# A causal convolution of five taps: diagonal matmuls in split precision, or matmuls by quarters of 32 channels over a copy folded through DRAM

## The chip, the cores and the metric

The kernel runs on one core of a Trainium2 chip. Its engines are TensorE (PE; the loads of its weights are shown apart as PEld), VectorE (DVE), ScalarE (ACT), GpSimd (POOL), and SyncE (SP), which here only issues DMA transfers. The metric is the time of one execution in microseconds, as the median of several runs. Lower is better.

## The reference

Three layers over 4 sequences of 576 positions and 512 channels, all in fp32:

```
attention   8 heads of 64; scores q k^T / 8; only the 32 highest scores of a row are kept; softmax; times v
first MLP   h = relu(x w_in); u, v = halves of h; v normalized over its channels
            v = w_spatial v + b_spatial (over the positions);  x = (u * v) w_out
second MLP  g[s,c] = sum over k<5 of conv_w[k,c] * x[s-4+k,c]      (zeros before the start)
            out = (sigmoid(g) * (x w_val)) w_out2
```

The change is in the line for g: 5 taps along the positions, each channel by itself.

## The kernel before

Attention goes in 72 units of two tiles of 128 rows, 18 units for each sequence. A unit computes its scores on PE in two halves (L475), ACT copies each half out of PSUM (L478), DVE searches for the 32nd highest score of each row (L494 to L529, the longest part of a unit) and masks and sums (L546), ACT scales (L521, L554), PE transposes (L563, L568), ACT copies (L565, L570), and PE multiplies by v (L584). Up to three units of scores are buffered (`sb`).

The two MLPs of sequence b, called MoE b below, are listed with the attention of sequence b+1, so that PE works on them while DVE works on attention. MoE 3 has no attention beside it: it is the tail. Weights come as 64-bit floats, which are decoded at the start on ACT, DVE and POOL and put as two fp32r parts (a high and a low part) into DRAM (`w_...`); they are loaded by POOL into `wblk` when they are needed, 2 MB at a time. A product is three matmuls in fp32r: high by high, high by low, low by high (L625). Activations are split likewise: the high part on ACT (L609), the low part on POOL (L611).

Order on each engine: everything is put into a list with its dependencies, an engine and an estimated duration (`od.add`). `Order.play` plays this list by a priority, `Order.plan` plays it first with hand-set lead times (`AHEAD`), and then `ROUNDS` times from the end and from the start, and takes the play that it believes the shortest. Each engine then runs its instructions in that fixed order. So a change of an estimate or a dependency anywhere moves instructions everywhere.

The convolution, for MoE 0 to 2: `x2` (the input, `piece_x2`) is in `UX` as [128 channels, 4 blocks d, 4 + 576 positions] and split into `yh` and `yl`. For each half c of the positions and each block d, PE multiplies 15 times (L777): the high part of a diagonal matrix of tap k by `yh` and `yl`, its low part by `yh`, for 5 taps. The 40 diagonals are made once on ACT (L291, `diagonals`), and take the buffer `diag`, which the last sequence uses for a weight (`w_load_late`). ACT takes tanh(g/2) from PSUM into `gate` (L780). MoE 3, in the tail, does the convolution on DVE instead (L788); that part does not change.

Of the kernel before, what the change touches and what calls it, by code (L numbers as in the profile page):

```python
# [39 lines left out]
class Order:  # L40
# [7 lines left out]
    ROUNDS = 4  # L48
# [159 lines left out]
def attention_moe_pass(tc, sh, fast, qT, kT, v, w_in, w_spT, b_sp, w_out, w_val, conv_w, w_out2, out):  # L208
# [17 lines left out]
    with ExitStack() as ctx:  # L226
# [50 lines left out]
        cwp = [buf(f"cwp{z}", [128, KK * TAPS], dt) for z, dt in enumerate((F32R, F32))]  # L277
        DIAG = buf("diag", [128, 2, KK * TAPS, 128], F32R)

        def diagonals(od, at):  # L280

            flat = cw.rearrange("p k t -> p (k t)")
            od.add("ACT", 0.2, lambda: nc.scalar.activation(cwp[0], flat, AF.Copy), [("cw",)], [("cwp", 0)], at)
            od.add("POOL", 0.3, lambda: nc.gpsimd.tensor_tensor(cwp[1], flat, cwp[0].bitcast(F32), op=ALU.subtract),
                   [("cw",), ("cwp", 0)], [("cwp", 1)], at)
# [19 lines left out]
        def decode(od, st, src, n, at, w=None, name=None, kk=0, c=0):  # L305
# [8 lines left out]
            od.add("SP", fn=lambda: nc.sync.dma_start(raw, src), w=[(k, 0)], at=at, **dma(1, 1024 * n))  # L314
# [62 lines left out]
        def decode_all(od, jobs, stages, t0, t1):  # L377
            m = 0
            for z, (name, src, c, n, kk) in enumerate(jobs):
# [9 lines left out]
                else:  # L389
                    words = src.bitcast(I32)[kk * 128:(kk + 1) * 128, 2 * c:2 * (c + n)].rearrange("p (n t) -> p n t", t=2)  # L390
                    to = dict(name=name, c=c % DM) if name else dict(w=cw[:, kk, :])
# [14 lines left out]
        def w_load_late(od, name, at):  # L406

            t = DIAG.rearrange("p z j c -> p (z j c)")
            WT[name] = (t, ("wlate",))
            od.add("POOL", 1.05, lambda: nc.gpsimd.dma_start(t[:, 0:WN[name]], sh.scratch[name]), [("scr", name)],  # L410
                   [("wlate",)] + [("diag", z, d) for z in range(2) for d in range(KK)], at, 9.0)

        def wpart(t, lo):
            n = KK * FF
            return t[:, lo * n:lo * n + n].rearrange("p (k f) -> p k f", k=KK)
# [178 lines left out]
        mp_n, vr_n, ga_n, os_n = [0], [0], [0], [0]  # L594
# [32 lines left out]
        def moe(od, b, t0, t1):  # L627
# [131 lines left out]
            GJ = {}  # L759

            def conv(c, d, at):
# [6 lines left out]
                if b < B - 1:  # L768
                    j = nxt(mp_n, banks)
                    ps = MP[j]  # L770
                    ky = [k for r in region("y", d * YW + c0, d * YW + c1 + PADC) for k in r]

                    def go():
                        ops = [(z, y, k) for k in range(TAPS) for z, y in ((0, "yh"), (0, "yl"), (1, "yh"))]
                        ops.sort(key=lambda o: o[0])
# [64 lines left out]
            if b == B - 1:  # L840
                w_load_late(od, "out", ("L", PER * B))
                od.add("-", 0.0, lambda: None, [], [("sps",), ("ptp", 0), ("ptp", 1), ("xr",)] + [("mp", j) for j in range(NMP, banks)])
# [158 lines left out]
```

## Time and profile before

| | before |
|---|---|
| median of 3 runs | 843.98 us (842.83 to 844.89) |
| the profiled execution | 839.99 us, of which the span is 838.1 us |
| DVE busy in the span | 754.7 us (90%) |
| PE busy | 708.3 us (85%) |
| ACT busy | 602.8 us (72%) |
| POOL busy | 290.6 us (35%) |

The profiled execution is 3.99 us below the median of the runs shown. The stages by the trace: decoding and attention of sequence 0 until about 225 us, MoE 0 to 2 each beside the attention of the next sequence until about 742 us, and the tail (MoE 3) until 838 us.

### The profile page before, as it was taken

The page shows a single profiled execution, that of the slowest core. Times are in us where ns is not written, and L with a number is a line of the kernel's source. Part 1 is how long each engine was busy: PE and PEld are TensorE (multiplying, and loading weights), DVE is VectorE, ACT ScalarE, POOL GpSimd, SP SyncE. Part 2 cuts the span into 40 slices and gives each one's busy share as a digit, 9 for nine tenths or more (in the row PEclk, how much of TensorE's full clock was granted, in tenths as well). Part 3 has the DMA queues.
Part 4 walks back from the last instruction along what each step waited for, and adds up shares of the span by engine and source line. Part 5 has one row for each costly group of instructions (what it writes and reads, how often), then busy time and mean ns, then how long its engine had stood idle before and what let it go on. Part 6 is the DMA issues. An engine that isn't in the chain of part 4 may idle for free.

```text
span 838.1 us, 17270 instructions
## 1 busy us (share of the span) xinstructions
PE 708.3 (85%) x5969; PEld 605.2 (72%) x5969; DVE 754.7 (90%) x2749; ACT 602.8 (72%) x1390; POOL 290.6 (35%) x353
## 2 busy tenths in 40 slices
PE   3245545755899999998999999997999999999986
PEld 2234433544789899876888899875888999778985
DVE  6999999999999999999999999998989999951580
ACT  5668866777887777768977777786886777774341
POOL 4767255564523311132442322232333112322120
PEclk9955666777999999999999999998999999999999
DMA  7888332323134502153133412234035003533601
GB/s 248 245 261 304 101 121 91 115 86 109 39 100 146 184 2 76 55 196 120 29 134 113 156 30 102 100 101 143 2 142 194 23 2 131 210 120 123 221 2 61
DMA packets 46954, 99.25 MB, mean 118 GB/s; under 512 B 22532, under 2 KB 29960, under 8 KB 43272
## 3 DMA queue, kind: packets, MB, share of 16 engines
q0 software_dynamic: 4032, 53.74, 18.1%
q1 hardware_dynamic: 42824, 44.31, 16.8%
q8 instruction: 49, 0.80, 0.4%
q14 instruction: 49, 0.40, 0.2%
HBM read 79.88 MB, written 18.15 MB: 117 GB/s over the span
## 4 chain that ended last, share of the span: by engine, by line
DVE 51%; PE 23%; ACT 6%; issue 2%; POOL 1%; DMA 0%; POOLq 0%; DVEq 0%; ACTq 0%
DVE tw L527 10%; DVE e L546 10%; PE mp L625 8%; DVE t8b L529 7%; PE mp L728 4%; DVE tm L494 4%; DVE cand L503 4%; DVE tm L495 3%; DVE cand L506 3%; PE xr L584 3%; DVE t8a L516 2%; DVE cand L498 2%; PE sps L475 2%; DVE tn L499 2%; DVE gate L788 2%
## 5 line engine op out<-in xcount | busy, mean ns | idle before, releaser
L475 PE MATMUL sps<-k,q 64*128 64x144 f32 (+1 forms) x1280 | 126.4, 341 | 85.2 <-ACT sb L478 77.9
L475 PEld LDWEIGHTS sps<-k,q 64*128 64x128 f32 (+1 forms) x1280 | 90.4, 201 | 116.0 <-ACT sb L478 88.6
L546 DVE SCALAR_TENSOR_TENSOR e<-sb,t8b,e 128x576 f32<-128x576 f32 x144 | 132.5, 945 | 0.1
L529 DVE MAX8 t8b<-tw 128x8 f32<-128x168 f32 x432 | 120.3, 318 | 0.0
L554 ACT ACTIVATE e<-e,sums 128x576 f32<-128x576 f32 x144 | 106.6, 770 | 9.5 <-DVE sums L551 9.3
L521 ACT ACTIVATE e<-sb,neg 128x576 f32<-128x576 f32 x144 | 106.5, 770 | 2.2 <-PE ptp L563 1.0
L478 ACT ACTIVATE sb<-sps 128x576 f32<-128x576 f32 x144 | 93.0, 646 | 19.6 <-PE sps L475 17.2
L563 PE MATMUL ptp<-ident,e 128*128 128x128 f32 x576 | 94.5, 301 | 11.1 <-ACT e L554 8.5
L584 PE MATMUL xr<-pt,vt 128*64 128x128 f32 (+1 forms) x1280 | 87.8, 281 | 18.0 <-ACT pr L570 17.7
L625 PE MATMUL mp<-xh,wblk 128*128 128x288 f32 x448 | 102.2, 306 | 0.0
L584 PEld LDWEIGHTS xr<-pt,vt 128*64 128x64 f32 x1280 | 68.3, 144 | 36.4 <-ACT pr L570 23.6
L563 PEld LDWEIGHTS ptp<-ident,e 128*128 128x128 f32 x576 | 72.0, 153 | 25.0 <-ACT e L554 13.1
L527 DVE MATCH_REPLACE8 tw<-t8b,tw 128x168 f32<-128x168 f32 x288 | 88.8, 314 | 0.0
L565 ACT ACTIVATE pt<-ptp 128x512 f32<-128x512 f32 x144 | 81.7, 596 | 8.4 <-PE ptp L563 8.1
L625 PEld LDWEIGHTS mp<-xh,wblk 128*128 128x128 f32 x448 | 74.6, 188 | 5.5 <-issue 1.2
L625 PE MATMUL mp<-wblk,xh 128*128 128x512 f32 (+1 forms) x280 | 73.9, 406 | 1.1 <-POOL stage L327 1.1
L494 DVE TENSOR_TENSOR tm<-sb 128x576 f32<-128x576 f32 x72 | 58.8, 817 | 5.6 <-ACT sb L478 5.4
L611 POOL TENSOR_TENSOR yl<-ux,yh 128x288 fp32r<-128x288 f32 x31 | 29.5, 953 | 94.9 <-ACT yh L609 92.5
L625 PE MATMUL mp<-xl,wblk 128*128 128x288 f32 x224 | 60.9, 294 | 0.0
L625 PEld LDWEIGHTS mp<-wblk,xh 128*128 128x128 f32 (+1 forms) x280 | 49.8, 186 | 14.9 <-POOL stage L327 1.3
L495 DVE TENSOR_TENSOR tm<-sb 128x576 f32<-128x576 f32 x72 | 60.4, 838 | 0.0
L503 DVE MAX8 cand<-tm 128x8 f32<-128x288 f32 x144 | 57.8, 441 | 0.0
(180 smaller groups left out, 1687.9 us busy)
## 6 DMA issues: line engine op xcount, KB each, us to landing
wblk<-w_out POOLq DMA_DIRECT2D x7, 2048.0 KB, 8.4
wblk<-w_sp POOLq DMA_DIRECT2D x8, 1440.0 KB, 6.5
wblk<-w_inv POOLq DMA_DIRECT2D x4, 2048.0 KB, 8.3
wblk<-w_inu POOLq DMA_DIRECT2D x4, 2048.0 KB, 9.1
wblk<-w_val POOLq DMA_DIRECT2D x4, 2048.0 KB, 9.0
q<-in_qT SPq DMA_DIRECT2D x16, 288.0 KB, 3.9
k<-in_kT SPq DMA_DIRECT2D x16, 288.0 KB, 4.4
stage<-in_w_in SPq DMA_DIRECT2D x8, 512.0 KB, 4.5
```

The lines of the kernel that those rows point to most:

```text
L475: nc.tensor.matmul(dst[:, f:f + QUART], lhsT=l, rhs=r[:, f:f + QUART], start=True, stop=True)
L478: od.add("ACT", t_actp(S), lambda c=c: nc.scalar.activation(sb[:, :, CH[c][0]:CH[c][1]], sps[:, :, 0:HALF], AF.Copy), [("sps",)], [("sb", ...
L494: tt(m[:, :, 0, :], sb[:, :, 0:HALF], sb[:, :, HALF:S], op=ALU.max)
L503: nc.vector.max(cand[:, t, QUART + 16:QUART + 24], m[:, t, 1, :])
L521: od.add("ACT", t_act(S, 1), lambda t=t: nc.scalar.activation(e[:, t, :], sb[:, t, :], AF.Exp, bias=neg[:, t:t + 1], scale=scale), ksb + [ ...
L527: nc.vector.match_replace(w[:, t, :], (t8a if r == 1 else t8b)[:, t, :], (src if r == 1 else w)[:, t, :], LOW)
L529: nc.vector.max(t8b[:, t, :], w[:, t, :])
L546: od.add("DVE", 0.85, lambda t=t, g=g: nc.vector.scalar_tensor_tensor(e[:, t, :], sb[:, t, :], t8b[:, t, 7:8], e[:, t, :], op0=ALU.is_ge, ...
L554: od.add("ACT", t_act(S, 1), lambda t=t, g=g: nc.scalar.activation(e[:, t, :], e[:, t, :], AF.Copy, scale=sums[:, g:g + 1]), [kg[t]], [("e ...
L563: nc.tensor.transpose(pp[:, j, :], e[:, t, REM * t + 128 * j:REM * t + 128 * j + 128], ident)
L584: nc.tensor.matmul(xr[64 * o:64 * o + 64, 2, 0:nq], lhsT=vt[:, kt, 64 * o:64 * o + 64], rhs=r, start=kt == 0, stop=kt == KT - 1)
L625: nc.tensor.matmul(ps, lhsT=l, rhs=r, start=m == 0, stop=m == len(ops) - 1)
```

## The change

For MoE 0 to 2 the convolution becomes matmuls in plain fp32 (no split). The 128 channels of a block are taken in quarters q of 32. In a new buffer `fold` the partitions hold 4 copies of the 32 channels of a quarter, copy r shifted by r positions, so one matmul over 128 partitions adds 4 taps for 32 channels; a second one adds the fifth tap (m = 1, shifted by 1, where only copy 3 has a weight). The weights `band` are [128, 32] blocks, 4 quarters by 2 for each d. Each quarter writes its own 32 partitions of one PSUM bank. `fold` is filled through DRAM: one DMA writes a block of `UX` into `lines`, four DMAs read it back, shifted. All five are issued by SP. The writes are listed with `piece_x2`, and the convolution a stage later than before. The convolution weights are decoded in one piece, replicated on 4 groups of partitions; `band` is made by POOL after the decoding; `ROUNDS` goes from 4 to 8. The last weight gets a buffer of its own in the room that `band` and `fold` leave.

```diff
@@ class Order
-    ROUNDS = 4
+    ROUNDS = 8
@@ attention_moe_pass
-        DIAG = buf("diag", [128, 2, KK * TAPS, 128], F32R)
+        NQR, NFOLD, FW = 4, 2, HALF + 1
...
@@ diagonals
-            for z in range(2):
-                part = cwp[z].bitcast(F32)
-                for d in range(KK):
-                    def go(z=z, d=d, part=part):
-                        for j in range(d * TAPS, (d + 1) * TAPS):
-                            nc.scalar.activation(DIAG[:, z, j, :], ident, AF.Copy, scale=part[:, j:j + 1])
-                    od.add("ACT", TAPS * 0.293, go, [("cwp", z)], [("diag", z, d)], at)
...
+            for d in range(KK):
+                def go(d=d):
+                    n = NQR * 2
+                    nc.gpsimd.tensor_tensor(
+                        BUF["band"][:, d].rearrange("p q m c -> p (q m) c"), ident4.unsqueeze(1).to_broadcast([128, n, 32]),
+                        coef[:, d].rearrange("p q m -> p (q m)").unsqueeze(2).to_broadcast([128, n, 32]), op=ALU.mult)
+                od.add("POOL", 0.8, go, [("coef",), ("cwn",), ("late",)], [("band", d)], at)
@@ decode
+                def load():
+                    for r in range(4):
+                        nc.sync.dma_start(t[32 * r:32 * r + 32, 0:2 * n].rearrange("p (x w) -> p x w", w=2 * TAPS), src)
+                od.add("SP", fn=load, w=[(k, 0)], at=at, **dma(4, 1024 * n))
@@ line_out (new)
+                od.add("SP", fn=lambda: nc.sync.dma_start(sh.lines[dj], UX[:, d, c0:c1 + PADC]),
+                       r=kux(d, c0, c1 + PADC), w=[("lines", dj)], at=at, **dma(1, 512 * YW))
@@ conv
+                    def load():
+                        for r in range(4):
+                            nc.sync.dma_start(BUF["fold", fj][32 * r:32 * r + 32],
+                                              lines[:, r:r + FW].rearrange("(q p) s -> p q s", p=32))
+                    od.add("SP", fn=load, r=[("lines", dj), ("late",)], w=[("fold", fj)], at=at, **dma(4, 512 * NQR * FW))
...
-                        for m, (z, y, k) in enumerate(ops):
-                            nc.tensor.matmul(ps[:, 0:HALF], lhsT=DIAG[:, z, d * TAPS + k, :],
-                                             rhs=BUF[y][:, d * YW + c0 + k:d * YW + c1 + k], start=m == 0, stop=m == len(ops) - 1)
-                    od.add("PE", 15 * 0.143, go, ky + [("diag", z, d) for z in range(2)], [("mp", j)], at)
+                        for m in range(2):
+                            for q in range(NQR):
+                                nc.tensor.matmul(ps[32 * q:32 * q + 32, 0:HALF], lhsT=BUF["band"][:, d, q, m, :],
+                                                 rhs=BUF["fold", fj][:, q, m:m + HALF], start=m == 0, stop=m == 1)
+                    od.add("PE", 2 * 0.6, go, [("fold", fj), ("band", d)], [("mp", j)], at)
@@ moe
+            if b < B - 1:
+                for d in range(KK):
+                    step(1.5, piece_x2, 0, d)
+                    step(0, line_out, 0, d)
+                for d in range(KK):
+                    step(1.5, piece_x2, 1, d)
+                    step(0, line_out, 1, d)
+                    step(0, conv, 0, d)
+                for d in range(KK):
+                    step(1.5, piece_val, 0, d)
+                    step(0, conv, 1, d)
```

What this makes of the engines' orders at three places. First PE in MoE 1, at the first convolutions. Before, after a half of scores and a product, one convolution stood as (the rest of the 15 alternate in the same way):

```order
L475 MATMUL sps<-k_90,q_86 128x144 x4
L568 MATMUL xr<-ident,e_101 128x128
L777 MATMUL mp_142<-yh,diag 128x288
L777 MATMUL mp_142<-yl,diag 128x288
L777 MATMUL mp_142<-yh,diag 128x288 x5
```

In the changed kernel two convolutions stand behind one another, after all products of the first half:

```order
L655 MATMUL mp_152<-xh,wblk_142 128x288 x4
L821 MATMUL mp_151<-fold_1763,band 32x288 x8
L821 MATMUL mp_150<-fold_1764,band 32x288 x8
L505 MATMUL sps<-k_98,q_94 128x144 x4
L593 MATMUL ptp_147<-ident,e_109 128x128 x4
```

Fifteen matmuls over 128 columns of weights have become eight over 32.

Second SP in MoE 0. Before, its queue held only loads of attention (and later stores of the output):

```order
L453 DMA vt_91<-in_v 128x4x64
L454 DMA vt_91<-in_v 64x64
L442 DMA q_83<-in_qT 128x576
L442 DMA k_87<-in_kT 128x576
L442 DMA q_84<-in_qT 128x576
L442 DMA k_88<-in_kT 128x576
```

Now the writes and reads of the convolution stand between them:

```order
L795 DMA lines_70<-ux 128x292
L795 DMA lines_71<-ux 128x292
L472 DMA q_91<-in_qT 128x576
L812 DMA fold_1763<-lines_70 32x4x289 x4
L795 DMA lines_72<-ux 128x292
L812 DMA fold_1764<-lines_71 32x4x289 x4
L795 DMA lines_73<-ux 128x292
L472 DMA k_95<-in_kT 128x576
L472 DMA q_92<-in_qT 128x576
```

Each line before the next has to be released first: a write waits for its `ux`, a `q` for a free buffer, a `fold` for its `lines` and for the convolution that used the buffer before.

Third PE where MoE 1 ends and MoE 2 begins (512 columns are output pieces of MoE 1 or first products of MoE 2; `sps` are halves of scores). Before, these stood behind one half of scores, and after them came ten products with v and the transposes of the next unit before the next half:

```order
L475 MATMUL sps<-k_87,q_83 128x144 x4
L625 MATMUL mp_144<-wblk_134,xh 128x512 x8
L625 MATMUL mp_144<-wblk_134,xl 128x512 x4
L563 MATMUL ptp_139<-ident,e_100 128x128 x4
L563 MATMUL ptp_140<-ident,e_100 128x128 x4
L568 MATMUL xr<-ident,e_100 128x128
L625 MATMUL mp_142<-wblk_134,xh 64x512 x8
L625 MATMUL mp_142<-wblk_134,xl 64x512 x4
```

Now there is at this point one piece of 512 columns for each half of scores:

```order
L655 MATMUL mp_151<-wblk_141,xh 128x512 x8
L655 MATMUL mp_151<-wblk_141,xl 128x512 x4
L505 MATMUL sps<-k_95,q_91 128x144 x4
L593 MATMUL ptp_147<-ident,e_109 128x128 x4
L598 MATMUL xr<-ident,e_109 128x128
L593 MATMUL ptp_148<-ident,e_109 128x128 x4
L655 MATMUL mp_152<-wblk_142,xh 128x512 x8
L655 MATMUL mp_152<-wblk_142,xl 128x512 x4
L505 MATMUL sps<-k_95,q_91 128x144 x4
```

The scores come earlier among the products. The last 342 rows of PE's order (the tail from the last attention on) are the same in both but for the names of buffers.

## Rows read from the trace of the kernel before

**Rows 1.** Windows by stage: us, then busy PE, PEld, DVE, ACT, POOL; clock, DMA, GB/s.

```profile
0.00:60.00 60.00, 20.98 (x126) 15.62 (x126) 50.60 (x135) 35.72 (x80) 39.19 (x44) 0.88 0.81 251
60.00:225.00 165.00, 97.92 (x772) 75.90 (x774) 159.89 (x587) 125.83 (x308) 87.56 (x89) 0.69 0.38 125
225.00:300.00 75.00, 74.87 (x697) 66.40 (x693) 73.95 (x289) 59.45 (x138) 26.67 (x35) 1.00 0.37 124
300.00:400.00 100.00, 96.53 (x845) 81.09 (x844) 99.03 (x388) 75.91 (x173) 20.00 (x24) 1.00 0.27 94
400.00:475.00 75.00, 72.53 (x671) 62.96 (x670) 74.35 (x277) 59.45 (x140) 29.07 (x40) 1.00 0.35 120
475.00:560.00 85.00, 83.59 (x760) 73.15 (x758) 85.00 (x333) 65.09 (x147) 20.55 (x20) 1.00 0.25 81
560.00:645.00 85.00, 79.62 (x681) 67.92 (x680) 77.02 (x287) 66.74 (x150) 27.22 (x42) 0.96 0.30 100
645.00:742.00 97.00, 96.72 (x855) 84.55 (x854) 96.97 (x385) 72.21 (x163) 21.32 (x25) 1.00 0.32 112
742.00:838.00 96.00, 85.55 (x579) 77.60 (x577) 37.88 (x78) 42.39 (x101) 19.01 (x36) 0.96 0.28 100
```

**Rows 2.** Waits of DVE, 560 to 645 us, then 0 to 225: total, times, longest.

```profile
DVE tm L494 <- ACT sb L478: 5.4, 3, 2.4
...
DVE stage L319 <- ACT stage L315: 7.1, 3, 5.1
```

**Rows 3.** Chain of waits, 574 to 600 and 280 to 300 us: start, length.

```profile
575.33 1.33 PE xr L584 x20
576.66 3.77 PE mp L625 x12
...
284.52 2.47 PE mp L777 x15
...
296.98 2.18 PE mp L777 x15
```

**Rows 4.** Timeline of PE, 232 to 288 us: start, length of the piece.

```profile
283.20 1.09 PE L584 MATMUL xr<-pt,vt 128*64 128x128 f32 x16
284.13 0.39 PE L584 MATMUL xr<-pr,vt 128*64 128x128 f32 x4
...
286.91 0.72 PE L475 MATMUL sps<-k,q 64*64 64x144 f32 x16
...
234.61 0.76 PE L475 MATMUL sps<-k,q 64*128 64x144 f32 x8
```

**Rows 5.** Line 584 by itself, 225 to 742 us: ns min/median/max.

```profile
L584 PEld LDWEIGHTS xr<-pt,vt x956: 132/137/227, 224.9 to 740.3; 128*64 128x64 f32 x192
```

**Rows 6.** Groups by line and shape: busy us, mean ns, idle before.

```profile
L291 ACT ACTIVATE diag<-ident,cwp 128x128 fp32r<-128x128 f32 x40 | 12.5, 395 | 0.0
...
L320 POOL TENSOR_TENSOR stage<-stage 128x256 fp32r<-128x256 f32 x24 | 22.1, 921 | 12.7 <-ACT stage L332 12.7
```

**Rows 7.** Timelines of DVE and POOL at 564 us; line 498 alone, ns min/median/max.

```profile
564.84 1.54 DVE L498 TENSOR_TENSOR cand<-tm 128x288 f32<-128x288 f32 x1
...
564.19 1.88 POOL L611 TENSOR_TENSOR yl<-vraw,yh 128x512 fp32r<-128x512 f32 x1 [2.27 <-ACT yh L609]
...
L498 DVE TENSOR_TENSOR cand<-tm x72: 430/440/1542, 17.9 to 729.7; 128x288 f32<-128x288 f32 x72
```

**Rows 8.** DMA issues: count, KB each, us to landing; queue 1: packets, MB, share.

```profile
q1 hardware_dynamic: 42824, 44.31, 16.8%
...
wblk<-w_val POOLq DMA_DIRECT2D x4, 2048.0 KB, 9.0
...
vt<-in_v SPq DMA_DIRECT2D x32, 128.0 KB, 2.5
...
out<-ost SPq DMA_DIRECT2D x4, 128.0 KB, 3.8
```

**Rows 9.** Timeline of SP at 239 us: start, length of the issue.

```profile
238.93 0.59 SPq L453 DMA_DIRECT2D vt<-in_v  x1
```

More of the change, by code (lines that the diff above doesn't have):

```diff
@@ new lines, in attention_moe_pass, with coefs @@
+        NW = KK * NQR * TAPS
+        NBAND = KK * NQR * 2 * 32
+        cwn = buf("cwn", [128, KK, TAPS])
+        coef = buf("coef", [128, KK, NQR, 2])
+        ident4 = buf("ident4", [128, 32])
+        def diagonals(od, at):
+            quarter = [slice(32 * r, 32 * r + 32) for r in range(4)]
+            def coefs():
+                nc.gpsimd.memset(coef, 0.0)
+                for r, rows in enumerate(quarter):
+                    nc.scalar.activation(cwn[rows], cw[rows, :, r, :], AF.Copy)
+                    nc.scalar.activation(ident4[rows, :], ident[rows, rows], AF.Copy)
+                    nc.scalar.activation(coef[rows, :, :, 0], cw[rows, :, :, r], AF.Copy)
+                nc.scalar.activation(coef[rows, :, :, 1], cw[rows, :, :, 4], AF.Copy)
+            od.add("ACT", 1.6, coefs, [("cw",)], [("cwn",), ("coef",)], at)
+            for d in range(KK):
[5 more added lines that the diff above has]
+                od.add("POOL", 0.8, go, [("coef",), ("cwn",), ("late",)], [("band", d)], at)
@@ L404, in w_load, with w_load_late, go @@
                    [("scr", name)], [("wblk", j)], at, 9.0)
-        def w_load_late(od, name, at):
-            t = DIAG.rearrange("p z j c -> p (z j c)")
+        def w_load_late(od, name, scope, at):
+            t = [None]
             WT[name] = (t, ("wlate",))
-            od.add("POOL", 1.05, lambda: nc.gpsimd.dma_start(t[:, 0:WN[name]], sh.scratch[name]), [("scr", name)],
-                   [("wlate",)] + [("diag", z, d) for z in range(2) for d in range(KK)], at, 9.0)
+            def go():
+                scope.close()
+                t[0] = pool("wlate", 1, side="right").tile([128, WN[name]], F32R, name="wlate")
+                nc.gpsimd.dma_start(t[0], sh.scratch[name])
+            od.add("POOL", 1.05, go, [("scr", name)],
+                   [("wlate",)] + [("band", d) for d in range(KK)] + [("fold", j) for j in range(NFOLD)], at, 9.0)
         def wpart(t, lo):
             n = KK * FF
+            t = t[0] if isinstance(t, list) else t
             return t[:, lo * n:lo * n + n].rearrange("p (k f) -> p k f", k=KK)
@@ L916, in late_buffers @@
                     BUF[name, j] = p.tile([128, w], F32, name=f"{name}{j}")
+            p = conv_room.enter_context(tc.tile_pool(name="conv", bufs=1, side="right"))
+            BUF["band"] = p.tile([128, KK, NQR, 2, 32], F32, name="band")
+            for j in range(NFOLD):
+                BUF["fold", j] = p.tile([128, NQR, FW], F32, name=f"fold{j}")
         attention(od, 0, PER)
@@ L927, in attention_moe_pass @@
             decode_all(od, jobs, st[0], 0, PER // 2)
-            jobs = [(None, conv_w, 0, TAPS, kk) for kk in range(KK)]
+            jobs = [(None, conv_w, 0, NW, 0)]
             jobs += [(n, w, c, CUT, kk) for n, w in (("out", w_out), ("val", w_val), ("out2", w_out2))
@@ L954, in attention_moe_kernel @@
         sh.again = keep.tile([1, 1], I32, name="again")
-        sh.conv = keep.tile([128, NP, conv_w.shape[1]], F32, name="cw")
+        sh.conv = keep.tile([128, NP, 4, conv_w.shape[1]], F32, name="cw")
         half = S // 2
@@ L959, in attention_moe_kernel @@
                                    ("out", 4096), ("val", 4096), ("out2", 4096))}
+        sh.lines = [dram.tile([128, half + conv_w.shape[1] - 1], F32, name=f"lines{j}") for j in range(8)]
         attention_moe_pass(tc, sh, True, *args)
```

60 lines of the change are left out of this document (33 added, 27 removed).

## The prediction, made before the changed kernel ran

> **What bounds the kernel now.** I read the busy times by stage first [rows 1]. From 225 to 742 us, beside MoE 0 to 2, two engines are full at once: of 517 us DVE is busy 506.32 (the sum over the six windows) and PE 503.86. ACT and POOL have room. In the tail from 742 us PE is busy 85.55 of 96 us and DVE 37.88. So until 742 us nothing can be won that is not idle time of DVE, since the change takes no work from DVE; and the tail is PE's. The idle time of DVE, stage by stage, is 9.40 us to 60 us, 5.11 to 225, then 1.05, 0.97, 0.65, 0, 7.98 and 0.03: in all 25.2 us, of which 10.7 stand beside the MoEs.
>
> Then the waits of DVE [rows 2]: in the one bad stretch, 560 to 645 us, it waits 5.4 us of 7.98 for ACT to copy scores, and the chain of waits shows what is behind that [rows 3]: from 575.33 us ten products with v (20 in the trace), then a piece of 12 matmuls that took 3.77 us. That is PE coming back after idle time (the granted clock of the stretch is 0.96 where the others have 1.00 [rows 1]) and then working off products ahead of the scores DVE needs. At the start DVE waits 7.1 us for the first decoded weights [rows 2], which the change doesn't touch.
>
> **The convolution on PE.** Before, one took 2.18 us on the chain (2.47 once) [rows 3]; there are 24. Afterwards one is 8 matmuls in plain fp32. In the trace a plain fp32 matmul is two records (a half of scores is listed as 4 and recorded as 8 [rows 4]), so it is 16 records of 288 columns on a quarter of the array (128 rows by 32 columns). No such shape is in the trace; two stand near it. The scores on 64 by 64 tiles, also a quarter, make 16 records of 144 columns in 0.72 us, where the same scores on 64 by 128 tiles make 8 in 0.76 [rows 4]: half the columns of weights, twice the records in the same time, so the tiles do run beside each other. At 45 ns for 144 columns, 16 of 288 take 1.44 us. The products with v, on half the array (128 by 64), run 20 records of 128 columns from 283.20 to 284.52 us [rows 4]: 66 ns each; if a quarter runs twice as densely again, 33 ns, or 74 for 288 columns, and 16 take 1.19 us. I take 1.3 us. The bounds are 1.19 and, if quarters share the array no better than halves do, 16 x 66 x 288 / 128 = 2.38 us. By 1.3, PE saves 24 x (2.18 - 1.3) = 21 us; by the bounds it saves 24 or loses 5.
>
> The Trainium skill speaks against this. "TensorE: Matmul & The Clock Gate", in Part 3 on what overlaps, says that a weight load runs beside matmuls in flight only if it goes to other rows of the array; all tiles of the new convolution take all 128 rows. The trace disagrees for 64 columns: 20 loads of 137 ns each [rows 5] would by themselves be 2.74 us, and load and product together took 1.32 [rows 4]. By the rule the convolution would be slower than before; that case is among the rivals, priced from the rows.
>
> **What those 21 us are worth.** PE's work is not what ends last wherever it is saved: from 300 to 560 us and from 645 to 742 us DVE is idle for 1.65 us together [rows 1]. What can come back is the 7.98 us in 560 to 645 and some of the 1.05 us in 225 to 300. The order speaks for it: where MoE 1 meets MoE 2, two pieces of 512 columns, two sets of transposes and the products with v stood between one half of scores and the next; now one piece stands between two halves. PE gets through MoE 1 earlier too, by 8 x 0.88 = 7 us. Against it: PE that is ahead idles, and what follows idle time runs at a lower clock, as at 576.66 us. I take 5 us of the 7.98 and 1 of the rest: **-6 us**. The bounds are 0 and -10.7.
>
> **Weights of the convolution.** 40 activations on ACT go (12.5 us busy [rows 6]) and 13 small ones come. ACT is busy 125.83 of 165 us there [rows 1], and DVE's waits up to 225 us are for the first weights, so I take 0; if ACT was what held DVE up, at most the 5.11 us of idle time. POOL gets four products of 128 x 256, 921 ns each by the nearest row [rows 6], 3.7 us, just when MoE 0 begins. POOL there has room, but a product on POOL stretches one on DVE: the one at 564.84 us took 1.54 us instead of 0.44 while POOL worked on `yl` [rows 7]. Four times up to 0.9 us is 3.7; most of DVE's instructions are searches, so I take **+1**, with 0 and +3.7 as bounds.
>
> The decoding of the convolution's weights now begins with 4 x 512 pieces of 40 bytes instead of 4 x 128, near the start, where the DMA share is 0.81 [rows 1]. At queue 1's mean of 16.8% x 16 x 838.1 us / 42,824 = 53 ns for a packet [rows 8], 1536 more are 81 us of one engine, 5 us of all sixteen. Ahead of them in the queue are the first four weight blocks and `q` and `k`, behind them blocks that DVE reaches only after its first units, so nearly all is hidden: **+0.5**, bounds 0 and +5.
>
> **The way through DRAM.** SP issues five DMAs for each convolution, 0.59 us each by the load of v [rows 9]: 120 in all, 71 us of SP, which is otherwise waiting. A read of 148 KB lands in about 2.5 us as v's 128 KB do, a write in up to 3.8 us as the output's 128 KB [rows 8]. The writes are listed a stage ahead, so the reads are what matters: there are two `fold` buffers, and a read can be issued only when the convolution before the last has finished; four issues and a landing are 2.4 + 2.5 = 4.9 us. Between a convolution and the next but one PE has at least a product of 12 matmuls (12/15 of 2.18, 1.7 us), the products with v (1.3), two halves of scores (1.5) and a convolution (1.3): 5.8 us. So it fits, with 0.9 us to spare. Queued behind the reads on SP stand `q`, `k` and `v` of units that are still two or more units off. For waits now and then I take **+0.5**; the bound above is the slow rival's.
>
> **The sum.** -6 + 1 + 0.5 + 0.5 = -4 us, against a profiled execution of 839.99 us (838.1 of it span), so 836 for a like one. That execution was 4 us below the median of the runs shown; the forecast is for a median, 843.98 - 4 = **840.0 us**. With the bounds that stay in this case it lies between 836 and 842.
>
> **The rivals.**
> 1. More comes back: all 10.7 us beside the MoEs, because PE always has the scores ready, and nothing of the rest is paid: 833. For it: PE had 13 us of idle time in 517 and gets 21 more. Against: part of DVE's wait follows its own chain (mask, scaling, transposes, products with v), which stays. 13%.
> 2. It hardly matters: DVE's idle time at the meeting of two MoEs comes from the dependency of the next MoE on the attention just ended, and only changes its place: 844, by the small costs up to 846. For it: DVE was full wherever convolutions stood. 15%.
> 3. Slower, by the reads of `fold`. POOL's 2 MB loads of the weights for `val` and the output fall into the time of the convolutions and take 9.0 us [rows 8]. If a read shares the DMA engines with one for its whole length, it lands in 9.0 us instead of 2.5; PE, whose order is fixed, waits 6.5 - 0.9 = 5.6 us, and scores and products with v wait behind the convolution. Six such loads are 34 us. It decides from the point where the waits exceed the 21 us saved; at the full price PE is 13 us longer, and as DVE has up to three units of scores buffered I count half: 850. Against it: the loads use the engines only part of that time, and the DMA share beside the MoEs is 0.25 to 0.37 [rows 1]. 17%.
> 4. The quarters don't run four at a time, or the loads of weights don't run beside them. At 2.38 us PE has 5 us more than before: 844 to 850. If 16 loads of 137 ns [rows 5] come on top of 1.3 us, a convolution takes 3.5 us, PE has 32 us more where it was full, and the time is 860 to 875. The latter is what the rule above would make of it; the rows for 64 columns exclude it there, so 3% for it and 5% for the former.
>
> **How the numbers follow.** My forecast has 47%, its edges included. About 0.2% (1.7 us) is what a measurement of this kernel can tell from no change. Faster than that: most of the forecast (45%), the first rival (13%), and 2% of the second: 60%. The same: the rest of the forecast, most of the second and some of the fourth: 18%. Slower: the third, the rest of the second and fourth: 22%. The range reaches down to the first rival, 832, and up to most of the third, 850; below it lie some 6%, above some 10%.
>
> **What would show it.** In the profile after: the new convolution as 16 records ending within 1.2 to 1.5 us of its start; PE's busy time lower by 15 to 24 us; DVE's idle time from 225 to 742 us down from 10.7 to about 5; the wait of L494 for ACT's copy mostly gone; no wait of PE for `fold` over 2 us; the tail as long as before, about 97 us after DVE's last mask. It would be wrong if PE waits for `fold` appear on the chain, if the convolution takes 2.2 us or more, or if DVE's idle time before 225 us grows by more than 2 us.

## The result, and the profile after

The changed kernel took 849.57 us (median, 849.08 to 851.07), the kernel before 843.81 us in the same comparison: a ratio of 1.0071, with an interval of 1.0053 to 1.0089. It is slower by 0.7%, where faster by 0.5% had been forecast. Its profiled execution took 849.08 us, its span 846.8.

The stages after, to be held against [rows 1] (the same columns; the last attention ends later, so the last row goes to 750 us, and the tail is left out):

```profile
0.00:60.00 60.00, 17.90 (x109) 13.87 (x109) 49.68 (x133) 34.35 (x77) 40.49 (x40) 1.00 0.82 253
60.00:225.00 165.00, 105.12 (x757) 79.94 (x757) 155.59 (x556) 115.13 (x264) 84.36 (x87) 0.76 0.38 127
225.00:300.00 75.00, 71.77 (x654) 63.19 (x651) 75.00 (x291) 59.22 (x138) 26.44 (x36) 0.98 0.34 113
300.00:400.00 100.00, 97.40 (x915) 76.35 (x915) 98.33 (x386) 80.21 (x185) 25.55 (x30) 1.00 0.56 159
400.00:475.00 75.00, 71.63 (x662) 63.31 (x661) 73.12 (x279) 57.97 (x134) 23.20 (x34) 0.98 0.36 122
475.00:560.00 85.00, 76.19 (x728) 58.60 (x728) 77.42 (x306) 59.00 (x134) 15.87 (x18) 0.94 0.53 144
560.00:645.00 85.00, 82.26 (x723) 68.74 (x721) 84.98 (x325) 69.73 (x158) 26.26 (x40) 1.00 0.29 102
645.00:750.00 105.00, 95.62 (x884) 76.09 (x881) 101.08 (x398) 75.00 (x170) 24.96 (x28) 0.97 0.55 168
```

Length less busy time is DVE's idle time. In 560 to 645 us it fell from 7.98 to 0.02 us: what the forecast counted on came in full. It came back in three other stretches: 9.41 us instead of 5.11 from 60 to 225, 7.58 instead of 0 from 475 to 560, 3.92 instead of 0.03 in the last attention. In the last two the DMA share, 0.25 and 0.32 before, is now 0.53 and 0.55.

The chain of waits of the changed kernel through the first convolutions of MoE 1, and one place of MoE 2 (start, length, what):

```profile
476.41 3.47 DMA lines<-ux
479.90 0.30 SPq L812
...
481.19 3.27 DMA fold<-lines
484.46 0.25 issue
484.71 2.15 PE mp L821 x16
...
496.58 1.15 PE mp L821 x16
497.75 0.30 SPq L812
...
499.23 8.41 DMA fold<-lines
507.64 0.14 issue
507.77 1.54 PE mp L821 x16
```

```profile
683.64 1.15 PE mp L821 x16
684.79 0.02 issue
684.81 0.32 SPq L812
...
686.24 10.06 DMA fold<-lines
696.29 0.09 issue
696.38 2.15 PE mp L821 x16
```

Read the two groups together. A convolution ends at 497.73 and again at 684.79 us; at once SP issues the reads into the buffer that this convolution has freed; the last read lands 8.41 and 10.06 us later; only then the convolution that stands in PE's order can run. At 484.71 us it is the way itself that is long: 3.47 us for the write, 1.3 for the four issues, 3.27 for the last read, with no 2 MB load under way. The wait of [rows 3] for late scores has become a wait for `fold`. The convolution itself takes 1.15 us where PE comes from work. Behind the waits that end at 484.71 and 696.38 us it takes 2.15 us, at a granted clock of 0.50 (1.2 GHz, the lower of the two levels), and behind the one that ends at 507.77 us 1.54, at 0.73.

The DMA view of the changed kernel from 680 to 700 us (packets, MB and share of the 16 engines by queue; then issues: count, KB each, median us to landing):

```profile
q1 hardware_dynamic: 2113, 2.18, 47.4%
q0 software_dynamic: 144, 2.10, 33.4%
...
wblk<-w_out POOLq DMA_DIRECT2D x1, 2048.0 KB, 11.4
fold<-lines SPq DMA_DIRECT2D x12, 144.5 KB, 10.1
```

Here a read lands in 10.1 us, not in the 2.5 us of v's load [rows 8], and the 2 MB load of `w_out` beside it in 11.4, where the median of such loads was 8.4 before. It is not so everywhere. All 96 reads of the kernel:

```profile
DMA to landing us min/median/max: 2.6/3.9/10.4
```

The trace has the landing of 53 of them. Reads issued while a `w_out` load is under way take 5.4 to 8.7 us in MoE 0, 8.2 to 8.5 in MoE 1 and 10.0 to 10.4 in MoE 2; all the others take 2.6 to 4.9. Over the whole span queue 1 went from 42,824 packets at 16.8% [rows 8] to

```profile
q1 hardware_dynamic: 61640, 62.17, 25.6%
```

which is from 141 to 217 us of all sixteen engines: 76 us more, 3.2 us for each of the 24 convolutions. Nothing in the sum had that term. A mean over a stage also hid where it falls: in the three stretches of 40 us in which most convolutions of a MoE stand, the DMA share was 0.22, 0.16 and 0.06 before and is 0.94, 0.76 and 0.72 now (same view, kernel before, then changed kernel):

```profile
300.00:340.00 40.00, 40.00 (x378) 35.99 (x376) 39.03 (x157) 29.90 (x72) 7.30 (x8) 1.00 0.22 69
480.00:520.00 40.00, 40.00 (x390) 36.04 (x390) 40.00 (x159) 31.56 (x71) 8.92 (x9) 1.00 0.16 45
660.00:700.00 40.00, 40.00 (x395) 36.52 (x393) 40.00 (x160) 31.60 (x74) 6.87 (x9) 1.00 0.06 12
```

```profile
300.00:340.00 40.00, 39.58 (x430) 31.25 (x428) 39.55 (x153) 31.66 (x76) 9.34 (x9) 1.00 0.94 231
480.00:520.00 40.00, 34.38 (x350) 25.35 (x353) 32.42 (x128) 25.20 (x58) 4.01 (x5) 0.91 0.76 192
660.00:700.00 40.00, 35.13 (x371) 27.39 (x370) 40.00 (x149) 28.91 (x69) 8.78 (x10) 0.96 0.72 194
```

The groups of the new convolution line (records and ns min/median/max; idle time of PE and of its weight loads before it, by what ended it), then the waits of PE alone (us, times, longest):

```profile
L821 PEld LDWEIGHTS mp<-fold,band x384: 106/109/178, 306.5 to 712.9; 128*32 128x32 f32 x192
L821 PE MATMUL mp<-fold,band x384: 402/406/688, 306.5 to 713.1; 128*32 128x288 f32 x192
...
  DMA fold<-lines: 12.5, 5
```

```profile
PE mp L821 <- DMA fold<-lines: 8.9, 4, 3.4
```

The 12.5 us count the wait before 696 us twice, for the weight loads (3.6) and for the matmuls (3.4). PE itself waited 8.9 us: 0.3, 2.7, 2.6 and 3.4.

Where the time goes unit by unit is seen from how much later each unit's first search of DVE starts than in the kernel before (us, of the profiled executions; 0 to 17 stand in the start, 18 to 35 beside MoE 0, 36 to 53 beside MoE 1, 54 to 71 beside MoE 2):

```
unit             4    16    20    28    44    48    52    56    60    68    71
changed        1.5   7.4   7.7   5.9   5.9  12.3  12.4   8.4   6.5   9.9   9.2
```

So there are two candidates for the loss: some 7 us in the start, where no convolution runs yet, and the waits for `fold` beside MoE 1 and MoE 2, with the forecast gain between them.

### The profile page after: what moved, and what is told of

The parts are those of the page before. It is cut to its first block, busy times and chain, and to the rows that moved or that the text cites. A ratio compares the mean times of both kernels' runs of the same rounds, so it can differ in the third digit from the quotient of the medians.

```text
span 846.8 us, 17499 instructions
## 1 busy us (share of the span) xinstructions
PE 704.6 (83%) x5993; PEld 578.5 (68%) x5993; DVE 755.7 (89%) x2747; ACT 592.1 (70%) x1351; POOL 288.4 (34%) x352
## 3 DMA queue, kind: packets, MB, share of 16 engines
q1 hardware_dynamic: 61640, 62.17, 25.6%
q0 software_dynamic: 4032, 53.74, 17.9%
## 4 chain that ended last, share of the span: by engine, by line
DVE 43%; PE 29%; ACT 11%; DMA 9%; issue 3%; POOL 3%; SPq 1%; DVEq 0%; POOLq 0%; ACTq 0%
PE mp L655 12%; DVE tw L557 8%; DVE e L576 7%; DVE t8b L559 5%; PE sps L505 3%; DVE tm L524 3%; PE xr L614 3%; DVE tm L525 3%; DVE cand L533 3%; PE ptp L593 3%; DMA fold<-lines 3%; PE mp L758 3%; DVE cand L536 2%; PE mp L821 2%; ACT e L584 2%
## 5 line engine op out<-in xcount | busy, mean ns | idle before, releaser
L505 PE MATMUL sps<-k,q 64*128 64x144 f32 (+1 forms) x1280 | 128.5, 345 | 98.1 <-ACT sb L508 91.0
L505 PEld LDWEIGHTS sps<-k,q 64*128 64x128 f32 (+1 forms) x1280 | 92.1, 204 | 133.6 <-ACT sb L508 104.5
L576 DVE SCALAR_TENSOR_TENSOR e<-sb,t8b,e 128x576 f32<-128x576 f32 x144 | 128.9, 921 | 0.0
L584 ACT ACTIVATE e<-e,sums 128x576 f32<-128x576 f32 x144 | 106.8, 769 | 11.2 <-DVE sums L581 10.7
L593 PE MATMUL ptp<-ident,e 128*128 128x128 f32 x576 | 99.7, 314 | 9.3 <-ACT e L584 7.5
L614 PE MATMUL xr<-pt,vt 128*64 128x128 f32 (+1 forms) x1280 | 94.0, 285 | 11.4 <-ACT pr L600 9.1
L614 PEld LDWEIGHTS xr<-pt,vt 128*64 128x64 f32 x1280 | 72.0, 146 | 33.9 <-ACT pr L600 15.2
L593 PEld LDWEIGHTS ptp<-ident,e 128*128 128x128 f32 x576 | 74.6, 159 | 27.3 <-ACT e L584 11.2
L595 ACT ACTIVATE pt<-ptp 128x512 f32<-128x512 f32 x144 | 81.9, 594 | 11.4 <-PE ptp L593 10.7
L655 PE MATMUL mp<-wblk,xh 128*128 128x512 f32 (+1 forms) x280 | 76.2, 415 | 0.0
L524 DVE TENSOR_TENSOR tm<-sb 128x576 f32<-128x576 f32 x72 | 62.1, 863 | 0.4 <-ACT sb L508 0.4
L525 DVE TENSOR_TENSOR tm<-sb 128x576 f32<-128x576 f32 x72 | 59.2, 823 | 0.0
L758 PE MATMUL mp<-wblk,yh 128*128 128x288 f32 x243 | 53.7, 306 | 0.5 <-DVE ux L763 0.5
## 6 DMA issues: line engine op xcount, KB each, us to landing
fold<-lines SPq DMA_DIRECT2D x96, 144.5 KB, 3.9
```

What stands on the lines that cost most here:

```text
L505: nc.tensor.matmul(dst[:, f:f + QUART], lhsT=l, rhs=r[:, f:f + QUART], start=True, stop=True)
L524: tt(m[:, :, 0, :], sb[:, :, 0:HALF], sb[:, :, HALF:S], op=ALU.max)
L525: tt(m[:, :, 1, :], sb[:, :, 0:HALF], sb[:, :, HALF:S], op=ALU.min)
L576: od.add("DVE", 0.85, lambda t=t, g=g: nc.vector.scalar_tensor_tensor(e[:, t, :], sb[:, t, :], t8b[:, t, 7:8], e[:, t, :], op0=ALU.is_ge, ...
L584: od.add("ACT", t_act(S, 1), lambda t=t, g=g: nc.scalar.activation(e[:, t, :], e[:, t, :], AF.Copy, scale=sums[:, g:g + 1]), [kg[t]], [("e ...
L593: nc.tensor.transpose(pp[:, j, :], e[:, t, REM * t + 128 * j:REM * t + 128 * j + 128], ident)
```

## The experiments

Each ran in five rounds beside the kernel before, whose median was 843.28 us in the first four, 841.93 in the next seven and 843.0 in the last. Ratios are to it.

**1. No way through DRAM.** The changed kernel's order on PE, DVE and ACT; `fold` is zeroed once, and neither written to `lines` nor read back, so the convolution's values are left out.

```diff
-                od.add("SP", fn=lambda: nc.sync.dma_start(sh.lines[dj], UX[:, d, c0:c1 + PADC]),
+                od.add("SP", fn=lambda: None,
...
-                        for r in range(4):
-                            nc.sync.dma_start(BUF["fold", fj][32 * r:32 * r + 32],
...
+                        pass
```

> The changed kernel with every engine's order kept, but no DMA of the convolution: the buffer fold is set to zero once, nothing is written to lines or read back, so the convolution's values are left out. Theory 1 (PE waits for the reads of fold, in MoE 1 and MoE 2): those waits go, DVE's idle time of 7.6 us in 475 to 560 us and of 3.9 us after 645 us shrinks to about 1, and the time is 838 to 842. Rival (the loss is all in the order of the start, the reads cost nothing): 848 to 850.

Measured: 839.15 us, ratio 0.9944 (0.9924 to 0.9963). Against the changed kernel's 1.0071 the transfers cost 1.27%, some 10.7 us. Without them the change is a gain of 4.7 us by the ratio, close to the forecast's 4. Queue 1 is back at 16.9% of its span. DVE's idle time of 7.58 us from 475 to 560 us is gone (85.00 of 85 busy), and so is that of 645 to 742 us. That answers the first candidate too: here the start was even later, 9.8 us at the 16th unit, and 0.7 us of it was left at the last.

**2. Four real buffers.** The same order on every engine, and the planner still believes in two; the buffers are taken in turn out of four.

```diff
-                            nc.sync.dma_start(BUF["fold", fj][32 * r:32 * r + 32],
+                            nc.sync.dma_start(BUF["fold", fb][32 * r:32 * r + 32],
...
-            for j in range(NFOLD):
+            for j in range(4):
```

> The changed kernel with the same order, but four buffers for fold instead of two, so that a read doesn't wait for the convolution before the last. If the reads are late because they wait for a buffer: 841 to 845, PE's waits for fold under 2 us. If they are late because the four reads of a convolution (592 KB) fill the DMA engines for as long as they take: 848 to 850, the same waits.

Measured: 845.8 us, just above the figure expected if buffers were the cause, ratio 1.0031 (1.0006 to 1.0057), with an unusual spread of 839.94 to 852.48 over 12 runs. The coupling through two buffers is part of the price, some 3.4 us of 10.7 by the ratios, whose intervals just touch. The waits did not fall under 2 us, as had been expected for this case: PE waited 7.3 us for `fold` instead of 8.9. The wait of 2.6 us near 507 us shrank to 0.3, while the one beside the `w_out` load of MoE 2 grew from 3.4 to 4.4.

**3. Fewer pieces for the convolution's weights.** They come in 128 pieces of 640 bytes in place of 2048 of 40, which permutes their values.

```diff
-                        words = words.rearrange("(x p) w -> p x w", p=32)
+                        words = words.rearrange("(p x) w -> p x w", p=32)
```

> The changed kernel with the same order, but the convolution's weights are read in 128 pieces of 640 bytes instead of 2048 of 40 (they come in another arrangement, so the convolution's values change). If the small pieces delay the start: the first 200 us lose 4 to 6 us less, 844 to 846. If the order of the start is what costs: 849 to 850.

Measured: 849.96 us, ratio 1.0067 (1.0044 to 1.009), the same as the changed kernel, and the first searches of units 4 to 71 within 3 us of its own. The small pieces cost nothing that can be measured.

**4. The old convolution in the new order.** The changed kernel's order, with 15 matmuls by diagonals for each convolution and no transfers. The diagonals are copies of the identity, so the taps are left out.

```diff
-                            for q in range(NQR):
-                                nc.tensor.matmul(ps[32 * q:32 * q + 32, 0:HALF], lhsT=BUF["band"][:, d, q, m, :],
...
+                        for m, (z, y, k) in enumerate(ops):
+                            nc.tensor.matmul(ps[:, 0:HALF], lhsT=DIAG[:, z, d * TAPS + k, :],
```

> The order of the changed kernel with the convolution of before in its places: 15 matmuls by diagonals (four copies of the identity stand for the diagonals, the taps' weights are left out), no DMA of the convolution. What this differs from before is the order. If the order costs the 6 us of the start and nothing else: 846 to 850, with DVE as late at 205 us as in the changed kernel. If the order is innocent: 842 to 845.

Measured: 856.25 us, ratio 1.0155 (1.0127 to 1.0183), above both figures that had been expected. In one and the same order the new matmuls, with what makes their weights, are 2.1% better than the old ones without a transfer (1.0155 to 0.9944; 856.25 - 839.15 = 17.1 us). So in an order planned for it the convolution's own change is worth 17 us; PE's busy time differs by 25.4 us (721.6 and 696.2). An order planned for a shorter convolution is 13 us worse than the old one when it has to carry the old one. One stretch of this kernel, with the old convolutions in the new order:

```profile
560.00:645.00 85.00, 81.96 (x714) 67.88 (x706) 85.00 (x323) 69.75 (x159) 24.55 (x36) 0.98 0.32 111
```

DVE is full where MoE 1 meets MoE 2 here as well: the 7.98 us of [rows 1] go with the new order, also without the shorter convolution.

**5. Only the listing a stage behind.** The kernel before, diagonals and all, with the convolution listed a stage later for MoE 0 to 2, planned anew.

```diff
+            if b < B - 1:
+                for d in range(KK):
+                    step(1.5, piece_x2, 0, d)
+                for d in range(KK):
+                    step(1.5, piece_x2, 1, d)
+                    step(0, conv, 0, d)
...
```

> The listing alone: the kernel before with its diagonals, but the convolution listed a stage behind its input as in the changed kernel. If what the listing does is to reshuffle all orders: a start that is a few us faster or slower than before, 841 to 851, with no cause in the convolution itself. If listing is neutral: 843 to 845.

Measured: 847.04 us, ratio 1.0055 (1.0035 to 1.0074). The listing, with the new order that comes of it, costs 0.5%. Its units were 1.7 us late at the 16th and 10.8 at the 44th.

**6 and 7. The order of the start.** In the first, the changed kernel's start (attention of sequence 0 and the decoding) is put in the order of the kernel before, by a table of planned times; in the second, the kernel before gets the changed kernel's start.

```diff
+START = (
+    "S146 S228 S1184 P533 A731 P799 A992 D1085 D1276 D1508 D1641 A1739 A1762 A1881 D1846 D2016 D2356 D2590 D2675 "
...
+            lead = dict(zip(START_IDS, START.split()))
...
+            best = self.play(key)
```

> The changed kernel, but attention of sequence 0 and the decoding of the weights are put in the order that the kernel before plans for them; behind them the changed kernel's own order. If the order of the start costs the 6 us that DVE is behind at 205 us: DVE within 2 us of the kernel before at 205 us, and 842 to 845 in all (the waits for fold stay). If the start loses time by what is new in it (the weights in one piece, small products on POOL): 848 to 850.

> The reverse: the kernel before, its convolution by diagonals kept, but the start in the order that the changed kernel plans. If the order of the start is the cause: DVE 5 to 8 us behind the kernel before at 205 us, 848 to 852 in all. If not: 842 to 845.

Measured: 855.81 us, ratio 1.0152 (1.0128 to 1.0176), and 861.46 us, ratio 1.0238 (1.0214 to 1.0261). How late each unit is:

```
unit                           4    16    20    28    44    48    52    56    60    68    71
changed                      1.5   7.4   7.7   5.9   5.9  12.3  12.4   8.4   6.5   9.9   9.2
changed, start of before    -0.9   0.8   3.1   1.3   3.5  10.2  12.7   7.4   3.9   9.3   8.7
before, start of changed     6.0   7.7   5.6   5.2   7.1   7.1   7.1   9.9   9.9   9.9  10.4
```

The lateness at the 16th unit goes and comes with the order of the start: 0.8 instead of 7.4, 7.7 in the kernel before. In the kernel before it stays: 10.4 at unit 71. In the changed kernel it does not cost 7 us at the end: the 6.6 us gained by unit 16 are gone by unit 52, and 0.5 us is left at unit 71. Both totals missed what was expected, since these kernels were slower after the last unit as well (from unit 68 to the end 129.4 us in the changed kernel and 134.2 with the other start, 130.6 in the kernel before and 138.9 with the other start). Imposing the table doesn't leave all the rest as it was: PE's order differs in places until 646 us in the changed kernel and until 458 us in the kernel before, and ACT's and DVE's until the tail. The totals are therefore no measure of the start.

**8. The planner told of the landing.** The changed kernel with two estimates set from its trace, and planned anew: 2.4 us of issue and 9 us to the landing, where the planner's own formula gave 2.56 and 3.24.

```diff
-                        r=kux(d, c0, c1 + PADC), w=[("lines", dj)], at=at, **dma(1, 512 * YW))
+                        r=kux(d, c0, c1 + PADC), w=[("lines", dj)], at=at, dur=0.6, lat=4.0)
...
-                     od.add("SP", fn=load, r=[("lines", dj), ("late",)], w=[("fold", fj)], at=at, **dma(4, 512 * NQR * FW))
+                     od.add("SP", fn=load, r=[("lines", dj), ("late",)], w=[("fold", fj)], at=at, dur=2.4, lat=9.0)
```

> The changed kernel with other estimates in its plan: a read of fold takes 9 us to land after 2.4 us of issue, a write of lines 4 us, near what the trace showed beside weight loads. The order changes everywhere by it. If the waits for fold come from a plan that believed in 3.2 us: PE's waits for fold under 3 us and the time 842 to 846, if the new order of the start is no worse. If the reads cost what they cost wherever they stand: 848 to 851.

Measured: 841.31 us, just under the 842 to 846 expected, ratio 0.9987 (0.9971 to 1.0004): 0.8% better than the changed kernel, and the same as before. PE waited 1.6 us for `fold` instead of 8.9, although the 16th unit was 9.9 us late here, later than in the changed kernel.

**9. A quarter of the bytes.** The changed kernel's order; each read brings 72 of its 289 columns in the same number of rows, the other columns are zero, so values are left out.

```diff
-                                              lines[:, r:r + FW].rearrange("(q p) s -> p q s", p=32))
+                                              lines[:, r:r + 72].rearrange("(q p) s -> p q s", p=32))
```

> The changed kernel in its own order; each read of a quarter brings only the first 72 of its 289 columns (288 bytes of 1156 in each row), so the same 96 reads with the same number of rows bring a quarter of the bytes; the other columns of the two buffers are zero, so the convolution's values are left out. Theory A (what costs is that the reads' 578 KB for a convolution share the DMA engines with the 2 MB weight loads): most of the 10 us that the reads cost comes back, 840 to 843 us, and a read near 690 us lands in under 6 us instead of 10.1. Theory B (what costs is the number of rows, or the issue on SP and the two hops, whatever the bytes): 847 to 850 us, and the landing stays near 10 us.

Measured: 839.85 us, ratio 0.9964 (0.9946 to 0.9982): the time of Theory A. Queue 1 from 680 to 700 us, then the landing of all 96 reads, and the chain at the place that stood at 683.64 to 696.38 us in the changed kernel:

```profile
q1 hardware_dynamic: 2304, 0.59, 16.3%
```

```profile
DMA to landing us min/median/max: 1.7/2.2/7.9
```

```profile
676.66 1.15 PE mp L821 x16
...
679.31 7.85 DMA fold<-lines
687.16 0.09 issue
687.25 1.18 PE mp L821 x16
```

Issue, rows and hops through DRAM stay; the bytes go, and with them all but 0.2% (0.9964 to 0.9944 of experiment 1) of the price. PE waited 1.9 us for `fold` instead of 8.9. The sign that Theory A gave for the landing came in part only. The median fell from 3.9 to 2.2 us, but reads issued beside a `w_out` load, which is the same 2 MB here, still landed in 5.6 to 7.9 us in MoE 1 and 2: at the place shown in 7.85 instead of 10.06. That was enough, because PE has 8.2 us of other work there: the wait fell from 3.4 to 1.2 us, and the one near 507 us went.

**10. The order of experiment 8 without the transfers.** The edit of experiment 1 in that order.

> The order of the kernel planned with 2.4 us for the four issues and 9 us for the landing, without the transfers to and from DRAM (the two buffers are zeroed once, so the convolution's values are left out). It says what the reads still cost where the planner gives them their measured time. Theory A (with the read listed early enough nothing waits for it): 839 to 841 us, within 2 us of that kernel's 841.3. Theory B (the transfers also take DMA time from the weight loads, whenever they are issued): 833 to 837 us.

Measured: 840.17 us, ratio 0.9967 (0.995 to 0.9985), against 0.9987 with the transfers: the transfers still cost about 0.2%, with intervals that overlap. Theory A: a read planned early enough costs next to nothing, though it moves the same bytes. The 833 to 837 us of Theory B did not come. Two planned orders differ in many places, and experiments 5 to 7 show that this alone can move the time by 0.5 to 2.4%; but the price of the transfers is here taken within one order, as in experiment 1, and it was 1.27% there. Without transfers the two orders are about equal (0.9967 and 0.9944).

**11. Landing times and four buffers, both known to the planner.**

```diff
-        NQR, NFOLD, FW = 4, 2, HALF + 1
+        NQR, NFOLD, FW = 4, 4, HALF + 1
```

on top of experiment 8.

> The same planner's figures (2.4 us for the four issues, 9 us for the landing) and four buffers of a quarter's windows in place of two, which the planner knows of, so that a read may be issued two quarters earlier. If the two buffers still hold the reads back: 836 to 839 us, faster than both kernels. If not: 840 to 842 us, as with two buffers. The convolutions then wait under 1 us in all for a read.

Measured: 838.87 us, ratio 0.9958 (0.9937 to 0.9978), faster than both kernels. Its idle time before the convolutions, and two of its stretches:

```profile
  DVE gate L849: 2.0, 2
  issue: 1.3, 8
  DMA fold<-lines: 0.3, 2
```

```profile
475.00:645.00 170.00, 164.85 (x1549) 134.24 (x1548) 168.87 (x653) 135.94 (x312) 47.66 (x60) 1.00 0.45 137
645.00:745.00 100.00, 96.95 (x889) 77.75 (x887) 98.21 (x386) 77.63 (x178) 25.63 (x32) 0.98 0.61 181
```

The weight loads wait 0.3 us for `fold` in all, the matmuls not at all, and DVE's idle time in 475 to 645 us is 1.13 us (7.58 + 0.02 in the changed kernel, 7.98 in the kernel before [rows 1]), with DMA shares as high as in the changed kernel. Reads issued beside a `w_out` load still take up to 11.1 us; they are issued early enough. The order was planned anew, so how much of the 0.3% against experiment 8 belongs to the buffers and how much to the order was not told apart.

**12. The start once more, with short reads.** Experiments 6 and 9 together, so that reads hardly bind.

> The changed kernel with the start (the first attention and the decode part) in the order of the kernel before, the rest in its own order, and with reads of the first 72 of 289 columns (the convolution's values are left out), so that the reads hardly bind. It is to be held against the kernel with the same short reads and its own start, 839.85 us. Theory A (the start's order costs its 4 to 7 us whenever the reads do not eat them): 833 to 836 us. Theory B (what the start loses is won back later whatever the reads do, so its order is worth nothing): 838 to 841 us.

Measured: 841.83 us, ratio 0.9984 (0.9965 to 1.0003), against 0.9964 with the changed kernel's own start: no faster, nearer to Theory B than to A and above both. By units:

```
unit                                       4    16    20    28    44    48    52    56    60    68    71
short reads                              1.5   7.5   9.4   7.9   6.7   4.9   5.3   1.3  -0.6  -0.8  -1.4
short reads, start of before            -1.1   1.3   3.1   1.3   2.9   5.7   7.4   2.2  -1.2  -2.0  -2.7
```

6.2 us of lead at unit 16 have shrunk to 1.3 at unit 71. The total is spoiled by the tail, as in experiment 6: the last products with v wait for ACT's copy longer here and come back at the lower clock (0.50 from 736.9 to 739 us, against 1.00 in experiment 9 from 735 to 737). PE in this kernel, then in that of experiment 9:

```profile
736.93 1.98 PE L679 MATMUL xr<-pt,vt 128*64 128x128 f32 x16 [5.26 <-ACT pr L665]
```

```profile
735.02 1.09 PE L614 MATMUL xr<-pt,vt 128*64 128x128 f32 x16 [2.08 <-ACT pr L600]
```

So in the changed kernel the start's order is worth about 1 us at the last unit, with long reads and with short ones. Why the later units catch up there and not in the kernel before was not tried.

With `ROUNDS` at 4 in the changed kernel, or at 8 in the kernel before, the order on every engine stays what it was.

## Why the prediction was wrong

**The way through DRAM (+0.5) is the step that failed.** It measured 10.7 us (experiment 1). The prediction made four mistakes in it. It took the landing of one read, 2.5 us from v's load, for that of four reads issued together: they took 2.6 to 4.9 us where nothing large ran beside them, and 8.2 to 10.4 beside the `w_out` loads of MoE 1 and 2. It gave them no time on the DMA engines at all; the trace has 3.2 us of all sixteen for each convolution with its write. It held the mean DMA share of the stages, 0.25 to 0.37, against the rival, where the stretches of the convolutions showed 0.06 to 0.22 before and 0.72 to 0.94 after. And it left the write out, as listed a stage ahead; at 484.71 us PE waits 2.7 us behind a write, with no load beside it. The PE work between a convolution and the next but one was not the mistake: 5.8 us had been set against a round trip of 4.9, and at the two long waits it was 7.5 and 8.2 us, but first issue to last landing took 9.9 and 11.5.

**The third rival was right** in its mechanism: reads beside a 2 MB load land in about the 9.0 us that it named, and PE waits. Experiment 9 shows that the bytes of the reads are most of the price, experiment 2 that the two buffers are a part. Its figure of 850 is near the result by luck. It had six loads cost PE 34 us, less 21 saved, and halved the rest. In the trace the three `w_val` loads land before the first reads, the three `w_out` loads cost 0.3, 2.6 and 3.4 us, the wait behind the write 2.7 more: 8.9 us in all; and PE's busy time fell by 3.7 us, not 21. It is also no property of the reads alone: with the landing estimated at 9 us the planner puts the convolution far enough behind its read, and almost nothing waits (experiments 8, 10 and 11).

**The convolution's time** was right in kind and a little too long: 1.11 us on the chain in steady work, where 1.3 was taken and 1.19 was the lower bound.

```profile
515.82 1.11 PE mp L821 x16
```

Sixteen loads of 109 ns, 1.74 us by themselves, went on inside those 1.11 us. The rule that the prediction weighed, in the Trainium skill's "TensorE: Matmul & The Clock Gate", Part 3, would have set them one behind another; the trace disagrees for 32 columns as for 64. PE's busy time fell by only 3.7 us, not 15 to 24 (708.3 to 704.6), though the convolutions saved 25.4 us in one and the same order (721.6 in experiment 4, 696.2 in experiment 1). The new order takes 13.3 us more with the old convolutions (708.3 to 721.6), and the transfers add 8.4 (696.2 to 704.6). The convolutions behind two of the waits, 2.15 us at the lower clock, are some 2 us of the 8.4; the rest was not followed up.

**The -6 us** came in its place: DVE's idle time where MoE 1 meets MoE 2 went from 7.98 to 0.02 us, and the wait for ACT's copies of scores there is gone. Of the two reasons given for it, the order did it: with the old convolutions in that order DVE is full there too (experiment 4). What hangs on the shorter convolution shows in the whole, 17 us in one order.

**The weights (+1 and +0.5).** The small pieces cost 0 (experiment 3). POOL's four products took 849 ns each, 921 forecast; their effect on DVE was not tried alone.

**What the prediction left out** is the order. It named a growth of DVE's idle time before 225 us as a sign of error, and it grew by 5.2 us, from 14.5 to 19.7, without any cost having been set for it. Experiments 6, 7 and 12 show the start's order to be the cause of the late units there, and 0.5 to 1.3 us of it to be left at the last unit of the changed kernel; in experiment 1, 0.7 us are left of 9.8. The listing a stage behind costs 0.5% by itself (experiment 5); how much of that remains with the short convolution was not told apart.

**The tail** was 96.3 us after DVE's last mask, 96.9 before: as forecast.

## What to carry to other kernels

Cost a transfer twice: its own landing, and what it takes of all DMA engines in the stretch where it stands, with its neighbours issued in the same microseconds; a share averaged over a stage says nothing on a burst. A landing matters only where it is longer than the work that the order puts in front of its use; so look at the few reads that are waited for, and not at the median. Where a planner sets the order, a wait that the trace shows longer than the planner's estimate is first mended in the estimate: two numbers took 0.8% back here, and the order planned with two more buffers was 0.4% faster than the kernel before. And a delay early in a kernel need not be one of its end: follow it unit by unit before charging it.

## What the runs showed of the hardware

The time of a queue grew with the bytes of its packets at the same number of packets: 61,640 packets of queue 1 took 25.6% of sixteen engines' span with 62.17 MB, and 20.6% with 51.50 MB in experiment 9. From 680 to 700 us, 2113 packets of 1032 bytes in the mean took 47.4%, 72 ns each; in experiment 9, where less of the 2 MB load falls into that window, 2304 of 256 bytes took 16.3%, 23 ns each. At 72 ns for 1032 bytes sixteen engines would move some 230 GB/s, an estimate; the 2 MB loads in queue 0 move 53.74 MB at 18.1% of the span before, some 354 GB/s.

A large load delayed small reads more than their own bytes did. Reads of 144.5 KB issued during a 2 MB load landed in 8.2 to 10.4 us in MoE 1 and 2 of the changed kernel, and with a quarter of the bytes (experiment 9) still in 5.6 to 7.9; in the changed kernel the longest without a load beside it took 4.9 us.

Sixteen records over all 128 rows and 32 columns of weights took 1.11 us in steady work, as dense as the bound from the 64-column rows said (1.19 us): twice as many columns at a time as on half the array.
